# One decode block on one core: head pairs with interleaved K and V loads and a softmax per pair, in place of a K stage, one softmax for all heads and a V stage

## The chip, the cores and the metric

One core of one Trainium2 chip runs the kernel. The metric is the device time of one execution in microseconds (us), read as the median of several runs.

TensorE (the matmul engine) is PE in the profile, its weight load PEld, VectorE is DVE, ScalarE is ACT, GpSimd is POOL and SyncE, which issues most DMAs, is SP.

## The reference, cut to what matters

One token (a row of 640 numbers) goes through attention over a window of 4,096 cached positions with 32 heads of 192, then through a gated MLP.

```python
h  = x + A(layernorm(x));   h2 = h + B(layernorm(h))
def A(x):                     # 32 heads, Dh = 192, W = 4096
    q = (x @ wq)              # wq: 640 x 6144
    p = softmax(q @ k.T * Dh ** -0.5)     # k, v: the last W rows of each head's cache
    return (p @ v) @ wo       # wo: 6144 x 640
def B(x):                     # w_in 640 x 1536, w_out 768 x 640
    z = gelu(x @ w_in); z1, z2 = halves(z)
    return (z1 * (layernorm(z2) * w_sp + b_sp)) @ w_out
```

K and V of the window are 100.7 MB of the 119.35 MB that must be read. Each byte is used once, and the DMA engines were busy 95.5% of the span (kernel before), so this is a problem of reading memory.

## The kernel before

Each K or V tile holds one head: partition p has 32 consecutive positions of 192 numbers, 12,288 bytes in one piece. VectorE multiplies the K tile by the query, TensorE adds up the products with an identity matrix as weights, and scores of all 32 heads are collected. Only then come one maximum, one exponential and one sum for all heads, and after that the V stage. K and V tiles share five buffers.

```python
KVB = 5
kvp = ctx.enter_context(tc.tile_pool(name="kv", bufs=KVB))
...                                                   # plan of loads: x, wq and all K, then wo and all V, then w_in, w_out
for h in range(H):
    ...
    nc.vector.tensor_tensor(out=prod[:], in0=kt[:], in1=q_bc[:, h:h + 1, :].to_broadcast([P, J, Dh]), op=ALU.mult)
    for t in range(NT):                               # 12 matmuls of 512 columns
        nc.tensor.matmul(psv, lhsT=ident_bf[:], rhs=prod[:, :, t * G:(t + 1) * G], ...)
    nc.scalar.copy(out=spart[:, :, h % HH, :], in_=psv.rearrange("p j g -> p g j"))
...                                                   # max over all heads, exp, sums
for h in range(H):
    for jj in range(J // 2):                          # 16 matmuls of 384 columns
        nc.tensor.matmul(pv[0:2, 0:2 * Dh], lhsT=E_all[:, h, 2 * jj:2 * jj + 2], rhs=vt[:, 2 * jj:2 * jj + 2, :], ...)
    ...                                               # scaling, transposes, wo
...                                                   # MLP: h_col, w_in, gelu, layernorm, w_out
```

Of the kernel before, what the change touches and what calls it, by code (L numbers as in the profile page):

```python
# [9 lines left out]
F32 = mybir.dt.float32  # L10
ALU = mybir.AluOpType
# [5 lines left out]
def kernel(  # L17
# [19 lines left out]
    J = W // P  # L37
    DC = D // P
    F = B_w_in.shape[-1]
# [3 lines left out]
    DA = P  # L43
    DB = Dh - P
    assert W % P == 0 and D % P == 0 and Fh % P == 0 and 0 < DB <= P
    scale = float(Dh) ** -0.5
    eps = 1e-5

    G = 512 // J
    NT = Dh // G  # L50
    HH = min(H, 512 // J)
    assert Dh % G == 0 and H % HH == 0
    HG = 8 if H % 8 == 0 else H
    HQ = 8 if H % 8 == 0 else H
    WQC = HQ * Dh
    QB = 512 if WQC % 512 == 0 else 384
    assert WQC % QB == 0

    kwin = A_k_cache[0, :, Sk - W:, :].rearrange("h (p j) d -> h p j d", p=P)
    vwin = A_v_cache[0, :, Sk - W:, :].rearrange("h (p j) d -> h p j d", p=P)  # L60
    wq_v = A_wq.rearrange("(c p) n -> p c n", p=P)
    assert Dh == 192 and H % 2 == 0
    PPG = HG // 2
    wo_r = A_wo.rearrange("(q p i) n -> p q (i n)", p=P, i=3)
# [3 lines left out]
    I32 = mybir.dt.int32  # L68
    KVB = 5
    const = ctx.enter_context(tc.tile_pool(name="const", bufs=1))  # L70
    small = ctx.enter_context(tc.tile_pool(name="small", bufs=2))
    kvp = ctx.enter_context(tc.tile_pool(name="kv", bufs=KVB))
    wqp = ctx.enter_context(tc.tile_pool(name="wq", bufs=2))
    wop = ctx.enter_context(tc.tile_pool(name="wo", bufs=6))
    NSB = H // HH
    psum = ctx.enter_context(tc.tile_pool(name="psum", bufs=5, space=bass.MemoryType.PSUM))
    assert NSB <= 2
    psacc = ctx.enter_context(tc.tile_pool(name="psacc", bufs=1, space=bass.MemoryType.PSUM))
    o2p = ctx.enter_context(tc.tile_pool(name="o2", bufs=3))
    kctx = ExitStack()  # L80
    prodp = kctx.enter_context(tc.tile_pool(name="prod", bufs=2))
    psS = kctx.enter_context(tc.tile_pool(name="psS", bufs=NSB, space=bass.MemoryType.PSUM))

    def bank():
        return psum.tile([P, 512], F32, tag="bank", name="bank")

    NQC = H // HQ
    NG = H // HG
    tiles = {}
    x_row = const.tile([1, D], BF16)  # L90

    def dma_x():
        nc.sync.dma_start(out=x_row[:], in_=A_x[0])

    def dma_wq(ci):
        t = wqp.tile([P, DC, WQC], BF16, tag="wq", name="wq_sb")
        nc.sync.dma_start(out=t[:], in_=wq_v[:, :, ci * WQC:(ci + 1) * WQC])
        tiles[("wq", ci)] = t

    def dma_k(h):  # L100
        t = kvp.tile([P, J, Dh], BF16, tag="kv", name="kt")
        nc.sync.dma_start(out=t[:], in_=kwin[h])
        tiles[("k", h)] = t

    def dma_v(h):
        t = kvp.tile([P, J, Dh], BF16, tag="kv", name="vt")
        if h == H - 1 and J % 8 == 0:
            JQ = J // 4
            for qq in range(4):
                nc.sync.dma_start(out=t[:, qq * JQ:(qq + 1) * JQ, :], in_=vwin[h][:, qq * JQ:(qq + 1) * JQ, :])  # L110
        else:
            nc.sync.dma_start(out=t[:], in_=vwin[h])
        tiles[("v", h)] = t

    def dma_wo(qi):
        t = wop.tile([P, 3 * D], BF16, tag="woR", name="woR")
        nc.sync.dma_start(out=t[:], in_=wo_r[:, qi, :])
        tiles[("wo", qi)] = t

    def dma_win(c):  # L120
        if c == 0:
            wmlp = ctx.enter_context(tc.tile_pool(name="wmlp", bufs=1))
            tiles["w_in"] = wmlp.tile([P, DC, F], BF16, name="w_in_sb")
            tiles["w_out"] = wmlp.tile([P, FHC, D], BF16, name="w_out_sb")
        nc.sync.dma_start(out=tiles["w_in"][:, c, :], in_=win_v[:, c, :])

    def dma_wout():
        nc.sync.dma_start(out=tiles["w_out"][:], in_=wout_v)

    plan = [("x", 0, dma_x), ("wq", 0, lambda: dma_wq(0))]  # L130
    for h in range(H):
        if (h + 4) % HQ == 0 and (h + 4) // HQ < NQC:
            ci = (h + 4) // HQ
            plan.append(("wq", ci, lambda ci=ci: dma_wq(ci)))
        plan.append(("k", h, lambda h=h: dma_k(h)))
    NPAIR = H // 2
    for h in range(H):
        if h % 2 == 0 and h // 2 < NPAIR - 1:
            plan.append(("wo", h // 2, lambda qi=h // 2: dma_wo(qi)))
        plan.append(("v", h, lambda h=h: dma_v(h)))  # L140
    plan.append(("wo", NPAIR - 1, lambda: dma_wo(NPAIR - 1)))
    for c in range(DC):
        plan.append(("win", c, lambda c=c: dma_win(c)))
    plan.append(("wout", 0, dma_wout))
    plan_pos = {(k, i): n for n, (k, i, _) in enumerate(plan)}
    issued = [0]

    def need(kind, idx, ahead=KVB - 1):
        upto = min(len(plan), plan_pos[(kind, idx)] + 1 + ahead)
        while issued[0] < upto:  # L150
            plan[issued[0]][2]()
            issued[0] += 1

    need("wq", 0, ahead=2)
# [4 lines left out]
    ident_bf = const.tile([P, P], BF16)  # L159
    make_identity(nc, ident_bf[:])  # L160
    ident_f = const.tile([P, P], F32)
    make_identity(nc, ident_f[:])
# [8 lines left out]

    wsp_bf = const.tile([P, 1], BF16)
    nc.scalar.dma_start(out=wsp_bf[:], in_=B_w_sp[0].to_broadcast((P, 1)))
    bsp_bf = const.tile([P, 1], BF16)
    nc.scalar.dma_start(out=bsp_bf[:], in_=B_b_sp.to_broadcast((P, 1)))
    wsp_h = const.tile([P, 1], F32)
    nc.vector.tensor_scalar(out=wsp_h[:], in0=wsp_bf[:], scalar1=0.5, scalar2=None, op0=ALU.mult)
    bsp_h = const.tile([P, 1], F32)
    nc.vector.tensor_scalar(out=bsp_h[:], in0=bsp_bf[:], scalar1=0.5, scalar2=None, op0=ALU.mult)

# [30 lines left out]
    def ln_stats(T, C, avg_mat, eps_, iters):  # L211
        return ln_stats_b(ln_stats_a(T, C, avg_mat), eps_, iters)

    xc_ps = bank()
    for c in range(DC):
        nc.tensor.matmul(xc_ps[:, c:c + 1], lhsT=x_row[0:1, c * P:(c + 1) * P], rhs=ones_bf[0:1, 0:1],
                         start=True, stop=True)
    x_col = const.tile([P, 2, DC], F32)
    nc.vector.tensor_copy(out=x_col[:, 0, :], in_=xc_ps[:, 0:DC])
    mean1, rstd1 = ln_stats(x_col, DC, avgD_f, eps, 3)  # L220
    xn_bc = const.tile([P, DC, P], BF16)
    nc.vector.tensor_scalar(out=xn_bc[:], in0=x_col[:, 0, :, None].to_broadcast([P, DC, P]), scalar1=mean1,  # L222
                            scalar2=rstd1, op0=ALU.subtract, op1=ALU.mult)

    q_bc = const.tile([P, H, Dh], BF16)
    q_flat = q_bc[:].rearrange("p h d -> p (h d)")

    def q_chunk(ci):
        need("wq", ci, ahead=2)
        wq_sb = tiles.pop(("wq", ci))  # L230
        for nb in range(WQC // QB):
            ps = bank()
            for c in range(DC):
                nc.tensor.matmul(ps[:, 0:QB], lhsT=xn_bc[:, c, :], rhs=wq_sb[:, c, nb * QB:(nb + 1) * QB],  # L234
                                 start=(c == 0), stop=(c == DC - 1))
            col0 = ci * WQC + nb * QB
            nc.scalar.activation(out=q_flat[:, col0:col0 + QB], in_=ps[:, 0:QB], func=ACT.Copy, scale=scale)  # L237

    spart = prodp.tile([P, G, HH, J], BF16, tag="spart", name="spart", bufs=1)
    S_banks = []  # L240
    q_chunk(0)
    for h in range(H):
        if (h + 4) % HQ == 0 and (h + 4) // HQ < NQC:
            q_chunk((h + 4) // HQ)
        need("k", h)
        kt = tiles.pop(("k", h))
        prod = prodp.tile([P, J, Dh], BF16, tag="prod", name="prod")
        nc.vector.tensor_tensor(out=prod[:], in0=kt[:], in1=q_bc[:, h:h + 1, :].to_broadcast([P, J, Dh]),  # L248
                                op=ALU.mult)
        ps = bank()  # L250
        psv = ps[:, 0:J * G].rearrange("p (j g) -> p j g", j=J)
        for t in range(NT):
            nc.tensor.matmul(psv, lhsT=ident_bf[:], rhs=prod[:, :, t * G:(t + 1) * G],  # L253
                             start=(t == 0), stop=(t == NT - 1))
        nc.scalar.copy(out=spart[:, :, h % HH, :], in_=psv.rearrange("p j g -> p g j"))  # L255
        if h % HH == HH - 1:
            s_ps = psS.tile([P, 512], F32, tag="s_ps", name="s_ps")
            sv = s_ps[:, 0:HH * J].rearrange("p (a j) -> p a j", a=HH)
            for g_ in range(G):
# [128 lines left out]
    for pr in stage2:  # L388
        pair_wo(pr)
# [96 lines left out]
```

## Time and profile before

The median was 302.01 us over the first 4 runs (301.91 to 303.8).

| | before |
|---|---|
| read from memory | 119.35 MB, 395 GB/s over the span |
| DMA engines busy | 95.5% of the span |
| PE, DVE, ACT busy | 74%, 46%, 14% |
| last load (w_out) landed | 293.95 us |
| h_col (input of the MLP) written | 290.06 us |
| end of the span | 301.9 us |

The page of the kernel before. The rows of digits and of GB/s have 40 equal slices of the span; the line of percentages after the DMA queue is the chain of waits, followed back from the last instruction, by engine; a group line gives line, engine, operation, output and inputs, shapes, count, then busy us and mean ns, then the engine's idle time before it and what ended it:

```profile
span 301.9 us, 3098 instructions
...
DMA  5999999999999999999998899999999999999970
GB/s 169 423 435 399 436 416 420 418 420 431 417 421 408 427 431 417 423 431 417 425 419 352 314 414 431 425 417 422 425 423 416 418 426 429 422 420 419 394 264 2
...
q1 hardware_dynamic: 16092, 119.35, 95.5%
...
DMA 61%; PE 22%; DVE 13%; ACT 1%; issue 1%; ACTq 0%; DVEq 0%
...
L248 DVE TENSOR_TENSOR prod<-kt,q_bc 128x6144 bf16<-128x6144 bf16 x32 | 107.2, 3358 | 28.6 <-DMA kt<-in_A_k_cache_dram 23.0
...
L371 PE MATMUL bank<-vt,E_all 128*2 128x384 bf16 x512 | 89.9, 331 | 17.7 <-DMA vt<-in_A_v_cache_dram 17.7
```

DMA is at nine tenths in nearly every slice, and its queue holds 95.5% of the engines' time. The product (L248) is the large work of DVE; the values (L371) are two fifths of PE's 223.8 us. The exceptions are the first slice, the two slices from 158 to 174 us (352 and 314 GB/s) and the end. DVE does its product only in the first half of the span, and PE its value matmuls only in the second.

The windows view of the same kernel (per stretch: busy us and count of each engine, granted PE clock, DMA share, GB/s) tells the hole from the rest:

```profile
core 0: us, PE busy (x) PEld busy (x) DVE busy (x) ACT busy (x) POOL busy (x), PEclk, DMA share, GB/s
4.00:140.00 136.00, 100.19 (x426) 40.88 (x426) 103.90 (x50) 23.55 (x40) 0.00 (x0) 0.99 1.01 420
140.00:176.00 36.00, 28.07 (x136) 12.27 (x136) 14.28 (x19) 5.04 (x9) 0.00 (x0) 0.91 0.93 383
176.00:280.00 104.00, 82.37 (x526) 39.84 (x524) 12.24 (x38) 11.01 (x27) 0.00 (x0) 1.00 1.01 422
```

The DMA engines are full before and after the softmax of all heads and 0.93 full around it. A share a little over 1 is read here as full (1.01 beside 420 GB/s), so the GB/s beside it may be a few per cent high.

The timeline of the tail (start us, length us, engine, line, operation, output and inputs, shapes, count, then idle time before it) shows the values of the last head and h_col:

```profile
285.32 2.76 PE L371 MATMUL bank<-vt,E_all 128*2 128x384 bf16 x16
...
290.06 0.16 DVE L397 TENSOR_TENSOR h_col<-attn_ps,x_col 128x5 f32<-128x5 f32 x1 [0.60 <-PE attn_ps L357]
```

The values of the last head end at 288.1 us and h_col comes 2 us later; the 11.85 us from h_col to the end are the MLP.

### The profile page before, as it was taken

Reading aid. Unit: us, or ns where it says so; the run is one execution under the profiler, and the core shown is the slowest. Engines: PE = TensorE matmul, PEld = TensorE weight load, DVE = VectorE, ACT = ScalarE, POOL = GpSimd, SP = SyncE. Lnnn points to the kernel's source line nnn. Section 1 sums busy time; section 2 is a strip of 40 time slices with the busy share of each in tenths; the row PEclk is TensorE's granted clock in tenths of the full one; section 3 lists DMA queues with packets and bytes.
Section 4 is the critical chain, followed back from the end, with each engine's and each line's share of the span. In section 5 each row is a group of like instructions: output and inputs, shape, how many; then the busy total and the mean of one; then the engine's idle time right before and its main releaser. Section 6 shows DMA issues by size and latency. Waiting matters only on the chain.

```text
span 301.9 us, 3098 instructions
## 1 busy us (share of the span) xinstructions
PE 223.8 (74%) x1267; PEld 101.4 (34%) x1267; DVE 139.3 (46%) x157; ACT 42.7 (14%) x83; POOL 1.1 (0%) x9
## 2 busy tenths in 40 slices
PE   1377676786888977777767999888777677886952
PEld 0133232232333422233222544434333333343541
DVE  2397488947997598999624111110111011101154
ACT  1021311112111211111101111110111011102100
POOL 1000000000000000000000000000000000000000
PEclk9999999998899999999995999999999999999985
DMA  5999999999999999999998899999999999999970
GB/s 169 423 435 399 436 416 420 418 420 431 417 421 408 427 431 417 423 431 417 425 419 352 314 414 431 425 417 422 425 423 416 418 426 429 422 420 419 394 264 2
DMA packets 16395, 119.55 MB, mean 396 GB/s; under 512 B 1788, under 2 KB 2557, under 8 KB 8317
## 3 DMA queue, kind: packets, MB, share of 16 engines
q1 hardware_dynamic: 16092, 119.35, 95.5%
q8 instruction: 10, 0.16, 0.2%
q10 hardware_dynamic: 288, 0.00, 0.0%
q14 instruction: 5, 0.03, 0.0%
HBM read 119.34 MB, written 0.00 MB: 395 GB/s over the span
## 4 chain that ended last, share of the span: by engine, by line
DMA 61%; PE 22%; DVE 13%; ACT 1%; issue 1%; ACTq 0%; DVEq 0%
DMA kt<-in_A_k_cache_dram 35%; DMA vt<-in_A_v_cache_dram 24%; PE bank L371 15%; DVE prod L248 9%; DMA bsp_bf<-in_B_b_sp_dram 3%; PE rowA L333 2%; PE s_ps L260 1%; PE bank L253 1%; PE bank L234 1%; PE bank L309 0%; DVE lnt L204 0%; PE attn_ps L348 0%; DVE Sm L280 0%; DVE lny L207 0%; ACT E_all L284 0%
## 5 line engine op out<-in xcount | busy, mean ns | idle before, releaser
L248 DVE TENSOR_TENSOR prod<-kt,q_bc 128x6144 bf16<-128x6144 bf16 x32 | 107.2, 3358 | 28.6 <-DMA kt<-in_A_k_cache_dram 23.0
L253 PE MATMUL bank<-prod,ident_bf 128*128 128x512 bf16 x384 | 89.7, 385 | 30.4 <-DVE prod L248 30.4
L371 PE MATMUL bank<-vt,E_all 128*2 128x384 bf16 x512 | 89.9, 331 | 17.7 <-DMA vt<-in_A_v_cache_dram 17.7
L253 PEld LDWEIGHTS <-ident_bf 128*128 128x128 bf16 x384 | 35.9, 99 | 84.0 <-DVE prod L248 38.7
L371 PEld LDWEIGHTS <-E_all 128*2 128x2 bf16 x512 | 41.9, 85 | 61.7 <-DMA vt<-in_A_v_cache_dram 21.7
L384 DVE SCALAR_TENSOR_TENSOR o<-bank,RB,o2a 2x192 bf16<-2x192 f32 x32 | 13.0, 405 | 60.9 <-ACT o2a L383 59.2
L255 ACT CAST spart<-bank 128x512 bf16<-128x512 f32 x32 | 18.7, 585 | 105.6 <-PE bank L253 105.6
L383 ACT ACTIVATE o2a<-bank,RA 2x192 f32<-2x192 f32 x32 | 13.2, 411 | 113.1 <-PE bank L371 113.1
L311 DVE CAST o_sb<-bank 128x3 bf16<-128x3 f32 x16 | 2.6, 164 | 49.6 <-PE bank L309 49.6
L234 PE MATMUL bank<-wq_sb,xn_bc 128*128 128x512 bf16 x60 | 15.4, 415 | 5.5 <-DVE xn_bc L222 5.5
L333 PE MATMUL rowA<-woR,o_sb 128*1 128x512 bf16 x42 | 12.9, 378 | 3.3 <-DVE o_sb L311 3.3
L234 PEld LDWEIGHTS <-xn_bc 128*128 128x128 bf16 x60 | 6.2, 105 | 13.9 <-DVE xn_bc L222 5.6
L237 ACT ACTIVATE q_bc<-bank 128x512 bf16<-128x512 f32 x12 | 7.2, 597 | 17.8 <-PE bank L234 17.8
L336 PE MATMUL rowB<-woR,o_sb 128*1 128x128 bf16 x42 | 9.2, 219 | 0.0
L260 PE MATMUL s_ps<-spart,ident_bf 128*128 128x512 bf16 x32 | 7.2, 379 | 1.4 <-ACT spart L255 1.4
L333 PEld LDWEIGHTS <-o_sb 128*1 128x1 bf16 x42 | 3.5, 82 | 8.2 <-DVE o_sb L311 4.4
L260 PEld LDWEIGHTS <-ident_bf 128*128 128x128 bf16 x32 | 3.1, 98 | 5.5 <-issue 2.0
L266 DVE TENSOR_REDUCE m<-s_ps 128x16 f32<-128x512 f32 x2 | 1.4, 686 | 7.2 <-PE s_ps L260 7.2
L309 PEld LDWEIGHTS <-o 2*128 2x128 bf16 x48 | 2.4, 100 | 5.5 <-issue 5.0
L309 PE MATMUL bank<-ones_bf,o 2*128 2x1 bf16 x48 | 3.7, 166 | 0.5 <-DVE o L384 0.5
L336 PEld LDWEIGHTS <-o_sb 128*1 128x1 bf16 x42 | 3.5, 83 | 0.1
L185 PE MATMUL bank<-x_col,avgD_f 128*128 128x10 f32 x2 | 0.6, 376 | 3.7 <-DVE x_col L182 3.7
(86 smaller groups left out, 36.9 us busy)
## 6 DMA issues: line engine op xcount, KB each, us to landing
kt<-in_A_k_cache_dram SPq DMA_DIRECT2D x32, 1536.0 KB, 19.1
vt<-in_A_v_cache_dram SPq DMA_DIRECT2D x31, 1536.0 KB, 18.1
wq_sb<-in_A_wq_dram SPq DMA_DIRECT2D x4, 1920.0 KB, 14.3
woR<-in_A_wo_dram SPq DMA_DIRECT2D x16, 480.0 KB, 18.3
w_in_sb<-in_B_w_in_dram SPq DMA_DIRECT2D x5, 384.0 KB, 8.3
vt<-in_A_v_cache_dram SPq DMA_DIRECT2D x4, 384.0 KB, 14.8
w_out_sb<-in_B_w_out_dram SPq DMA_DIRECT2D x1, 960.0 KB, 9.9
wsp_bf<-in_B_w_sp_dram ACTq DMA_DIRECT2D x1, 0.2 KB
```

Source lines behind the costliest of these rows:

```text
L234: nc.tensor.matmul(ps[:, 0:QB], lhsT=xn_bc[:, c, :], rhs=wq_sb[:, c, nb * QB:(nb + 1) * QB], start=(c == 0), stop=(c == DC - 1))
L237: nc.scalar.activation(out=q_flat[:, col0:col0 + QB], in_=ps[:, 0:QB], func=ACT.Copy, scale=scale)
L248: nc.vector.tensor_tensor(out=prod[:], in0=kt[:], in1=q_bc[:, h:h + 1, :].to_broadcast([P, J, Dh]), op=ALU.mult)
L253: nc.tensor.matmul(psv, lhsT=ident_bf[:], rhs=prod[:, :, t * G:(t + 1) * G], start=(t == 0), stop=(t == NT - 1))
L255: nc.scalar.copy(out=spart[:, :, h % HH, :], in_=psv.rearrange("p j g -> p g j"))
L260: nc.tensor.matmul(sv, lhsT=ident_bf[:], rhs=spart[:, g_], start=(g_ == 0), stop=(g_ == G - 1))
L309: nc.tensor.matmul(o3_ps[:, i:i + 1], lhsT=o2f[:, i:2 * Dh:3], rhs=ones_bf[0:2, 0:1], start=True, stop=True)
L333: nc.tensor.matmul(rowA[0:1, 0:DA1], lhsT=pr["o3"][:, i:i + 1], rhs=woR[:, i * D:i * D + DA1], start=st_, stop=sp_)
L336: nc.tensor.matmul(rowB[0:1, 0:D - DA1], lhsT=pr["o3"][:, i:i + 1], rhs=woR[:, i * D + DA1:(i + 1) * D], start=st_, stop=sp_)
L371: nc.tensor.matmul(pv[0:2, 0:2 * Dh], lhsT=E_all[:, h, 2 * jj:2 * jj + 2], rhs=vt[:, 2 * jj:2 * jj + 2, :], start=(jj == 0), stop=(jj == J ...
L383: nc.scalar.activation(out=o2a[:], in_=pv[0:2, 0:Dh], func=ACT.Copy, scale=RA[:, h:h + 1])
L384: nc.vector.scalar_tensor_tensor(out=cur["o2"][:, hp, :], in0=pv[0:2, Dh:2 * Dh], scalar=RB[:, h:h + 1], in1=o2a[:], op0=ALU.mult, op1=ALU ...
```

## The change

The intent was to keep DMA full from start to end: give every stage the same mix of K and V work, close the hole at the softmax and use larger packets. Two heads share a tile (even partitions one head, odd partitions the other), so a row has 64 positions and 24,576 bytes. K and V loads alternate, K two pairs ahead. A manual schedule fixes the order of instructions: value work of pair t-2 stands after scores, maximum and exponential of pair t. The output projection uses 240 small matmuls in place of row matmuls, and the loads of w_sp and b_sp move from the start to the end. The diff, cut to its core:

```diff
-    kwin = A_k_cache[0, :, Sk - W:, :].rearrange("h (p j) d -> h p j d", p=P)
+    def pairs_of(cache, t):
+        return cache[0, 2 * t:2 * t + 2, Sk - W:, :].rearrange("h (p j) d -> p h (j d)", p=HALF)
-    wq_v = A_wq.rearrange("(c p) n -> p c n", p=P)
+    wq_v = A_wq.rearrange("(p c) n -> p (c n)", c=DC)
-    KVB = 5
+    KVB = 6
+    ctx.enter_context(tc.manual_schedule())
...
+    for t_ in range(NP):
+        if t_ + 2 < NP:
+            plan.append(("kv", lambda t=t_ + 2: dma_pair("k", A_k_cache, t)))
+        if t_ % 2 == 1:
+            plan.append(("wo", lambda q=t_ // 2: dma_wo(q)))
+        plan.append(("kv", lambda t=t_: dma_pair("v", A_v_cache, t)))
...
+    for t in range(NP + 2):
+        if t < NP:
+            S, m = scores(t)                 # 24 matmuls, 2 reductions
+        if ob_prev is not None:
+            columns(t - 3, ob_prev)
+        if t >= 4 and t % 2 == 0:
+            project((t - 4) // 2)
+        if t < NP:
+            gm = head_max(m)                 # transpose on PE, maximum on DVE
+            Z = exps(t, S, gm)               # broadcast on PE, exp on ACT
+        if t + 1 < NP:
+            for ch in range(NCH):
+                product(t + 1, ch)           # in place in the K tile
+        if t > 1:
+            ...
+            values(t - 2, vt, pv, 0, NJ)     # 32 matmuls
+            free("kv")
+            ob_prev = scaled(t - 2, pv)
+        if t < NP:
+            norms(t, Z)
...
+    nc.scalar.dma_start(out=wsp_bf[:, 0:1], in_=B_w_sp[0:1])     # was at the start
```

## The prediction

> **What bounds it now.** The DMA engines. By the windows view they are busy 0.99 of 4 to 140 us and 1.00 of 176 to 286 us, at 420 and 421 GB/s; the page gives 119.35 MB and 95.5% of 16 engines' span. DVE (46%) and PE (74%) are not the limit on average. DMA is not full in three places. First packets come 3.3 us after the start. Around 158 to 173 us (352 and 314 GB/s in the slices) the softmax of all heads runs alone and V buffers stay held: about 3.4 us of DMA is lost. After the last packet (about 293.4 us) 8.5 us of MLP follow; h_col is written at 290.06, 11.85 us before the end.
>
> **What the change does.** It handles heads in pairs (one on even, one on odd partitions), interleaves K and V loads and does a softmax per pair. Bytes stay the same, packets grow: a K or V row is 24,576 B, not 12,288; wq goes from 3,072 to 24,576 B, wo from 3,840 to 7,680.
>
> **Costs from the trace.**
> - Packets: the median 12,288 B packet took 464 ns, 3,072 B 125, 3,840 B 151. These fit 12 ns plus 27.2 B/ns [...]. Estimate for 24,576 B: 916 ns. Summed over 16 engines: 285 us before, 280 after: 4 to 5 us saved.
> - The softmax gap closes: 3.4 us saved.
> - Per pair, DVE: two products of 3.36, two PSUM reductions of 0.69, small ones 1.8: 9.9 us. PE: 24 score matmuls at 0.23, 32 value matmuls at 0.176, 1.2 for the rest: 12.5 us. The chain product, last scores, max, exp takes about 12.7. A pair's K and V take 14.7 us (17 with wo), and six buffers hold four loads ahead. So compute hides; DVE busy rises to about 155 us at no cost.
> - Start: q needs all of wq (21 us), then 80 matmuls, about 17 us; three K loads are in flight until 43 us, so DMA should not starve.
> - Tail, worse: value work lags two pairs. From the last K's landing (about 249 us): product 6.7, scores and softmax to 11.8, values 13, 14, 15 at 5.5 each with 1 to 2.5 us of scaling and projection between: to 32; h_col at 35, as late as the last DMA byte (34.6), where before it was 3.3 us ahead. The two tiny w_sp and b_sp loads move to the end of the scalar queue, ahead of h_col: 0 to 1.5 us more. In all 3 to 4 us given back.
>
> **Sum.** 302.0 - 4.5 - 3.4 - 0.8 (earlier first packet) + 3.5 = 296.8 us, range 293.5 to 300.5. Chances: faster by over 2% 0.40, within 2% 0.56, slower 0.04.
>
> **Signs.** DMA share 0.99 from 4 to 283 us without a hole in the middle, at 425 to 429 GB/s; K and V packets of 24,576 B at about 916 ns; last packet near 284 to 285 us; the chain of waits mostly DMA, with the last product and PE values at the end; h_col at about 285; PE waits 0 to 1.5 us for the w_sp load; 11 to 12 us from h_col to the end.
>
> **What would make it wrong.** Rows split into smaller packets, or no better rate for large ones: about 300. Two heads at once slowing HBM. A per-pair chain over 15 us (slow in-place product, PE waiting in program order for norms or transposes), so buffers come free late and DMA shows holes: 300 or more. A tail that overlaps better than I count: 294.

The two medians give both figures: from 3,072 B in 125 ns to 12,288 B in 464 ns it is 339 ns for 9,216 B, or 27.2 B/ns, and 12 ns are left over. The 916 ns stand on these alone.

## The result, and the profile after

The changed kernel took 300.92 us (median of 11 runs, 300.42 to 302.62), against 302.8 us for the kernel before (median of 16 runs, the first 4 among them). The ratio is 0.9951, 95% interval 0.9933 to 0.9968, a gain of about half a per cent. Ratios here are the mean time of one kernel's fast runs over that of the other's fast runs of the same rounds, so they are not quite the ratio of the medians. The predicted 296.8 us was too low by 4.1 us, and 300.92 lies just above the range. The time of a run is its span plus 1.7 to 1.9 us in every recorded run but one (2.1).

Lines of the page of the changed kernel: the span, the granted PE clock in tenths (PEclk), the GB/s, the DMA queue, the engines' shares of the chain of waits, and the groups of the product and the values:

```profile
span 298.9 us, 3737 instructions
...
PEclk9999995868999799989977998999989977999965
...
GB/s 306 431 421 444 434 426 429 420 431 437 417 425 440 423 441 424 423 437 420 431 437 414 434 431 417 437 431 421 418 444 423 434 431 427 428 421 398 293 2 0
...
q1 hardware_dynamic: 7930, 119.35, 94.0%
...
PE 64%; DMA 20%; DVE 12%; issue 1%; ACT 1%; SPq 0%; ACTq 0%; DVEq 0%
...
L240 DVE TENSOR_TENSOR k_t<-k_t,q 128x6144 bf16<-128x6144 bf16 x32 | 106.0, 3352 | 30.7 <-DMA k_t<-in_A_k_cache_dram 30.7
...
L292 PE MATMUL pv_ps<-v_t,E 128*4 128x384 bf16 x512 | 98.5, 358 | 0.0
```

The windows view of the changed kernel, same columns as before:

```profile
4.00:140.00 136.00, 103.53 (x587) 50.58 (x587) 76.76 (x104) 11.38 (x41) 0.00 (x0) 0.91 1.01 430
140.00:176.00 36.00, 33.54 (x215) 17.01 (x216) 23.89 (x30) 3.35 (x15) 0.00 (x0) 0.91 1.00 428
176.00:280.00 104.00, 88.56 (x627) 45.22 (x625) 54.05 (x77) 7.71 (x32) 0.00 (x0) 0.93 1.00 424
```

The product has kept its 3.4 us, in place or not; a value matmul takes 358 ns in the mean instead of 331. The hole is gone (1.00 and 428 GB/s where it was 0.93 and 383), and the rate is higher (430 GB/s from 4 to 140 us where it was 420). The DMA side of the prediction holds. In the packet records, packets of 24,576 B took 914 ns (median), where 916 was estimated. The w_out load landed at 284.31 us, 9.6 us earlier than before; the terms for DMA summed to 8.7. Of the 0.9 us more, 0.7 can lie at the start: the first packet of a large load came at 1.8 us instead of 3.3, where a gain of 0.8 was counted.

But from that landing to the end of the span it is now 14.6 us, where it was 8.0 us. So the tail gave back 6.6 us, not 3.5. The timeline of the changed kernel from the last but one K on:

```profile
235.47 6.63 DVE L240 TENSOR_TENSOR k_t<-k_t,q 128x6144 bf16<-128x6144 bf16 x2 [4.53 <-DMA k_t<-in_A_k_cache_dram]
...
238.88 7.03 PE L250 MATMUL sc_ps<-k_t,ident_bf 128*128 128x512 bf16 x24 [3.89 <-DVE k_t L240]
...
248.84 7.04 PE L292 MATMUL pv_ps<-v_t,E 128*4 128x384 bf16 x32
...
250.10 6.63 DVE L240 TENSOR_TENSOR k_t<-k_t,q 128x6144 bf16<-128x6144 bf16 x2
...
255.84 5.35 PE L250 MATMUL sc_ps<-k_t,ident_bf 128*128 128x512 bf16 x24
...
263.19 5.36 PE L292 MATMUL pv_ps<-v_t,E 128*4 128x384 bf16 x32
...
271.18 5.36 PE L292 MATMUL pv_ps<-v_t,E 128*4 128x384 bf16 x32
...
278.03 5.36 PE L292 MATMUL pv_ps<-v_t,E 128*4 128x384 bf16 x32
...
286.30 0.15 DVE L364 TENSOR_TENSOR h_col<-attn_ps,x_col 128x5 f32<-128x5 f32 x1
```

Read it as a chain on PE. The last K (pair 15) landed at 250.07 us by the landing records, and the first half of its product was done near 253.4. Yet its scores began at 255.84, because PE was still at the values of pair 12. From then on scores and three groups of values follow each other with gaps of 1.5 to 2.6 us, in which PE does small matmuls and waits for a maximum or a scaling. The last V landed at 277.01 us, and its values ended only at 283.4.

Two groups in these lines lasted about 7.0 us where their siblings took 5.36. The windows view of the changed kernel, same columns, in stretches of the length of the clock record's steps, shows why (the granted clock follows the counts of POOL):

```profile
235.80:239.20 3.40, 0.32 (x2) 0.19 (x2) 3.40 (x2) 0.00 (x0) 0.00 (x0) 0.99 1.06 455
239.20:242.60 3.40, 3.40 (x10) 1.22 (x8) 3.37 (x4) 0.00 (x0) 0.00 (x0) 0.51 0.94 405
...
246.00:249.40 3.40, 2.28 (x49) 1.83 (x48) 1.45 (x5) 0.20 (x1) 0.00 (x0) 1.00 0.97 411
249.40:252.80 3.40, 3.40 (x13) 1.33 (x12) 2.80 (x2) 0.57 (x4) 0.00 (x0) 0.50 1.06 447
```

After 3.4 us with 0.32 us of PE work, and again after 3.4 us with 2.28 us of it, the granted clock fell to half for the next 3.4 us; 5.36 us plus half of 3.4 us is 7.06 us, and the two groups took 7.03 and 7.04. Of the eleven half clock stretches in the clock record of this trace seven last 3.4 us and three 6.8 us; the last, from 286.9 us, runs to the end of the span. Why the clock falls was not shown. The mean granted clock was 0.967 before and 0.906 after.

### The profile page after: what moved, and what is told of

Read it like the earlier page. It is cut to its first block, busy times and chain, and to the rows that moved or that the text cites. A ratio compares the mean times of both kernels' runs of the same rounds, so it can differ in the third digit from the quotient of the medians.

```text
span 298.9 us, 3737 instructions
## 1 busy us (share of the span) xinstructions
PE 235.5 (79%) x1596; PEld 120.2 (40%) x1596; DVE 164.4 (55%) x266; ACT 24.7 (8%) x92; POOL 2.3 (1%) x10
## 4 chain that ended last, share of the span: by engine, by line
PE 64%; DMA 20%; DVE 12%; issue 1%; ACT 1%; SPq 0%; ACTq 0%; DVEq 0%
PE pv_ps L292 27%; PE sc_ps L250 26%; DMA k_t<-in_A_k_cache_dram 13%; DMA wq_t<-in_A_wq_dram 7%; PE sc_ps L226 5%; DVE k_t L240 3%; DVE S L252 3%; PE attn_ps L322 2%; PE sm_ps L267 2%; DVE gm L262 1%; PE sm_ps L260 1%; DVE m L255 1%; PE sm_ps L312 1%; DVE o L314 1%; ACT E L273 1%
## 5 line engine op out<-in xcount | busy, mean ns | idle before, releaser
L240 DVE TENSOR_TENSOR k_t<-k_t,q 128x6144 bf16<-128x6144 bf16 x32 | 106.0, 3352 | 30.7 <-DMA k_t<-in_A_k_cache_dram 30.7
L250 PE MATMUL sc_ps<-k_t,ident_bf 128*128 128x512 bf16 x384 | 90.7, 395 | 13.2 <-DVE k_t L240 13.2
L292 PE MATMUL pv_ps<-v_t,E 128*4 128x384 bf16 x512 | 98.5, 358 | 0.0
L292 PEld LDWEIGHTS <-E 128*4 128x4 bf16 x512 | 45.7, 92 | 46.7 <-issue 15.1
L252 DVE TENSOR_REDUCE S<-sc_ps 128x32 f32<-128x512 f32 x32 | 22.0, 688 | 41.7 <-PE sc_ps L250 41.7
L226 PE MATMUL sc_ps<-wq_t,xn 128*128 128x384 bf16 x80 | 17.6, 390 | 14.9 <-DMA wq_t<-in_A_wq_dram 14.9
L273 ACT ACTIVATE E<-S,bias 128x64 bf16<-128x64 f32 x32 | 11.2, 359 | 140.8 <-DVE bias L269 140.8
L226 PEld LDWEIGHTS <-xn 128*128 128x128 bf16 x80 | 9.1, 114 | 23.1 <-issue 16.0
L312 PEld LDWEIGHTS <-ob 4*32 4x32 bf16 x192 | 7.5, 134 | 9.4 <-issue 5.5
L312 PE MATMUL sm_ps<-sel,ob 4*32 4x1 bf16 x192 | 8.9, 184 | 3.0 <-DVE ob L300 3.0
```

Source lines behind the costliest of these rows:

```text
L226: nc.tensor.matmul(psv, lhsT=xn2[:, c, a, :], rhs=wc[:, 2 * gq:2 * gq + 2, a, :], start=(c == 0 and a == 0), stop=(c == DC - 1 and a == 1))
L240: nc.vector.tensor_tensor(out=kc, in0=kc, in1=q2[:, t:t + 1, :].to_broadcast([P, JC, Dh]), op=ALU.mult)
L250: nc.tensor.matmul(psv, lhsT=ident_bf[:], rhs=k3[:, ch * JC:(ch + 1) * JC, n * G:(n + 1) * G], start=(n == 0), stop=(n == NT - 1))
L252: nc.vector.tensor_reduce(out=S[:, ch * JC:(ch + 1) * JC], in_=psv, axis=AX.X, op=ALU.add)
L273: nc.scalar.activation(out=E[:, :, a], in_=S[:], func=ACT.Exp, bias=bias[:, a:a + 1], accum_out=Z[:, a:a + 1])
L292: nc.tensor.matmul(pv[0:4, 0:2 * Dh], lhsT=E[:, 2 * jj:2 * jj + 2, :], rhs=v2[:, jj, :], start=(jj == 0), stop=(jj == J // 2 - 1))
```

## The experiments

Two theories of the 4 us were on the table. The first: DMA paces the kernel up to the last loads, as predicted, and the loss sits in the tail, made of PE's program order and of half clock. The second, suggested by the chain view (PE 64%, DMA 20%): PE now paces the whole kernel, and the larger packets and the closed hole are worth nothing. A third suspicion was a wrong anchor, since the profile of before came from the slowest of its 16 runs. All runs were correct. They were made on three chips, each beside the kernel before, so they are best compared by their ratios.

### 1. The kernel before, once more (before_again)

No edit.

> The unchanged kernel of before, run again to learn its spread. Theory (wrong anchor): the profile of before that the prediction was computed from has a span of 301.9 us and came from a run timed at 303.8 us, while the median was 302.0 us; measured time is the span plus 1.8 us, so most runs of before should show spans near 300.2 to 301, and the predicted span of 296.8 us should have been quoted as 298.6 us. Rival (no anchor error): spans of before cluster at 301.9 us and the 303.8 us run is the odd one.

Measured: median 303.11 us of 4 runs, 302.29 to 303.38; ratio 1.0019, interval 0.9991 to 1.0046. Its spans were 300.5 to 301.6, and the kernel before, run beside it, had times of 301.48 to 303.55 us (11 runs). So the theory holds in its main point: time is span plus 1.8 or 1.9 us in each of these runs, and a span of 301.9 (time 303.8) is at the slow edge. The expected 300.2 to 301 was a little narrow. What makes one run of before slower than another by 1 to 2 us was not settled.

### 2. Small packets (small_packets)

```diff
-            nc.sync.dma_start(out=t[:], in_=src)
+            for a, b in ((J // 4, J // 2), (J // 2, 3 * J // 4), (3 * J // 4, J), (0, J // 4)):
+                nc.sync.dma_start(out=t[:, a * Dh:b * Dh], in_=src[:, :, a * Dh:b * Dh])
```

> Changed kernel with every K and V load cut into four DMAs of 6,144 B rows, the first quarter loaded last so that nothing can start earlier. Packets of 6,144 B took 236 ns and of 24,576 B 914 ns in the changed kernel, so a row costs 30 ns more and all rows 7.5 us more over 16 engines. If the DMA stream still paces the kernel up to the last K, the time rises by 6 to 7.5 us over the changed kernel (to about 307.5 us). If the chain of waits is right that PE (64%) now paces it, the time rises by under 2 us.

Measured: 307.09 us, ratio 1.0157 (1.0126 to 1.0188). Against the ratio of the changed kernel, 0.9951, that is 2.1% or 6.2 us more. Two lines of the page of this run, the GB/s and the DMA queue:

```profile
GB/s 310 422 414 412 418 421 416 421 413 419 415 418 419 412 418 415 416 417 417 416 417 416 418 417 416 417 417 416 417 421 412 417 420 415 418 421 415 351 11 0
...
q1 hardware_dynamic: 21322, 119.35, 95.4%
```

The rate fell to about 417 GB/s, and w_out landed at 291.62 instead of 284.31 us. So DMA still paces the kernel up to the last loads, and the second theory falls. The chain view gave PE 64% because it goes back from a load's landing to its issue, and from there to the PE work that freed the buffer. The one K load on that chain was issued at 196.33 us and landed at 235.44. It did not transfer for 39 us (at 430 GB/s its 3.1 MB take 7.3 us, by estimate): it stood in a full queue (DMA share 1.01 in that time). The same view gives softmax_late2 below DMA 55% and PE 30%, with loads that land at the same times.

### 3. Keeping PE busy in the tail (warm_tail)

```diff
+    def warm_pe(n):            # n dummy matmuls of 384 columns into a spare bank
+        wb = bank()
+        for _ in range(n):
+            nc.tensor.matmul(wb[:, 0:2 * Dh], lhsT=ident_bf[:], rhs=q2[:, 0:2, :], start=True, stop=True)
     for t in range(NP + 2):
+        if t == NP - 2:
+            warm_pe(22)
         if t < NP:
             S, m = scores(t)
+        if t >= NP:
+            warm_pe(5)
         if ob_prev is not None:
             columns(t - 3, ob_prev)
+        if NP - 2 <= t < NP:
+            warm_pe(5)
```

> Changed kernel with dummy matmuls in TensorE's idle stretches of the last four iterations (22 before the scores of pair 14, 5 in each later gap), the result unchanged. Theory (half clock matters): the scores of pair 14 and values of pair 12 ran at half clock (7.0 instead of 5.3 us) after idle stretches; with TensorE kept busy both run at 5.3 us and the time falls by 1.2 to 2 us. Rival (the order of the work alone sets the end, or the idle time is swallowed by waits): change under 0.4 us.

Measured: 299.39 us, ratio 0.9901 (0.988 to 0.9922), so 0.5% or 1.5 us less than the changed kernel. Its timeline has the dummies, the values of pair 12, and h_col:

```profile
235.81 3.75 PE L332 MATMUL sm_ps<-q,ident_bf 128*128 128x384 bf16 x22
...
248.24 5.36 PE L292 MATMUL pv_ps<-v_t,E 128*4 128x384 bf16 x32
...
285.24 0.15 DVE L376 TENSOR_TENSOR h_col<-attn_ps,x_col 128x5 f32<-128x5 f32 x1
```

The values of pair 12 took 5.36 us, not 7.04, and h_col came 1.06 us earlier, although the last K landed 0.4 us later (250.48 us). From that landing to h_col it is 34.8 us, where the changed kernel took 36.2. The clock record has no half clock between 220.1 and 285.0 us. Added PE work made the kernel faster. So half clock on the tail's chain cost about 1.5 us.

### 4. Deferring the softmax, first attempt (softmax_late)

In each iteration `values(t - 2)` was put ahead of columns, projection and maximum of pair t, and `exps` of pair t was moved to iteration t+1. The diff here and the next one are shortened to the calls.

```diff
         S, m = scores(t)
+        Z, E = exps(t - 1, ...)
+        product(t + 1)
+        nc.vector.tensor_copy(out=Z[:, 2:4], in_=Z[:, 0:2])
+        values(t - 2); scaled(t - 2)
         columns(t - 3); project(...)
-        gm = head_max(m); Z = exps(t, S, gm)
-        product(t + 1)
-        values(t - 2); scaled(t - 2)
-        norms(t, Z)
+        head_max(m)
+        norms(t - 1, Z)
```

> Changed kernel with another order of work in an iteration, no work added or taken: values of pair t-2 follow the scores of pair t at once on TensorE, and max, bias and exp of pair t are finished one iteration later, so TensorE has no wait of 2 to 3 us between scores and values. Theory (the tail is TensorE's backlog from waits in program order): values of the last pair end near 279.5 us instead of 283.4, h_col near 282.3 instead of 286.3, and the time falls by 3 to 4.5 us to about 297 us. Rival (the tail is bound by loads landing, last V at 277.0 and w_in at 281.9 us): under 1 us.

Measured: 303.98 us, ratio 1.0061 (1.0029 to 1.0093): 3 us slower than the changed kernel, so a miss. Its timeline shows the fault:

```profile
242.18 0.16 DVE L342 COPY Z<-Z 128x2 f32<-128x2 f32 x1
...
242.39 0.19 PE L279 MATMUL sm_ps<-ones_f,Z 128*4 128x1 f32 x2 [4.61 <-DVE Z L342]
...
242.51 8.09 PE L250 MATMUL sc_ps<-k_t,ident_bf 128*128 128x512 bf16 x24
```

The copy of Z (line 342) stood on DVE behind both products of pair 14, and PE's matmul for the norm (line 279), which needs it, stood ahead of the scores. So the scores began at 242.51 us, where the changed kernel began them at 238.88. Here two engines with a fixed order each made a wait of 4.61 us that neither order shows alone. The run tells nothing for or against the theory.

### 5. The same, with the order mended (softmax_late2)

```diff
         S, m = scores(t)
+        norms(t - 2, ...)          # needs a copy of Z made an iteration ago
+        columns(t - 3, ob_prev)
+        exps(t - 1, ...)
+        product(t + 1); copy of Z(t - 1)
+        values(t - 2); scaled(t - 2)
+        project(...)
+        head_max(m)
```

> The reordering of softmax_late, with its own fault mended: there the copy of Z stood behind the two products of the next pair on VectorE, and TensorE's matmul for the norm, which waits for that copy, stood ahead of the next scores, so the scores of pair 14 began at 242.5 instead of 238.9 us, after both products. Here norm and head columns of earlier pairs come right after the scores, nothing that TensorE does before the next scores waits for a product. Theory (order of work on TensorE makes the tail): scores of pair 15 end near 260 us, the last values near 279.5 us, h_col near 282.5 us, time 296 to 298 us. Rival (any deferral of the softmax costs as much as it gains, or the end is bound by landings): 300 us or more.

Measured: 297.62 us, ratio 0.9833 (0.9816 to 0.985), which is 1.2% or 3.6 us under the changed kernel by the ratios. Its timeline has the second half of the scores of pair 15, the values of pair 15 and h_col, near the expected 260, 279.5 and 282.5 us:

```profile
256.70 2.75 PE L250 MATMUL sc_ps<-k_t,ident_bf 128*128 128x512 bf16 x12 [0.52 <-DVE k_t L240]
...
274.30 5.36 PE L291 MATMUL pv_ps<-v_t,E 128*4 128x384 bf16 x32
...
282.58 0.15 DVE L371 TENSOR_TENSOR h_col<-attn_ps,x_col 128x5 f32<-128x5 f32 x1
```

The bytes, the arithmetic and the loads are the same; w_out landed at 284.45 us, as before the reordering (284.31), and the last K at 250.00 (250.07). So the order of work on PE in the tail, with the half clock on its chain, cost the changed kernel over 3 us. If half clock is put at the 1.5 us of warm_tail, the order alone is worth about 2 us, by estimate.

### 6. Tiny loads back to the start (late2_tail)

```diff
     nc.scalar.dma_start(out=x_row[:], in_=A_x[0])
+    nc.scalar.dma_start(out=wsp_bf[:, 0:1], in_=B_w_sp[0:1])          # and b_sp; was ahead of h_col
...                                # the negated mean computed inside the statistics, h2a ahead of the last c3
```

> softmax_late2 with the two tiny loads of w_sp and b_sp back at the start and two small VectorE instructions of the MLP tail moved into gaps. By the trace of the changed kernel TensorE waited for no tiny load (h_col 0.2 us after the last projection), and the MLP tail was 0.6 us longer than before by the order of small instructions: expected 0.3 to 0.8 us less than softmax_late2. If the tiny loads were a real cost at the tail, as the prediction allowed: 1 to 1.5 us less.

Measured: 297.05 us, ratio 0.9813 (0.9797 to 0.9829), 0.6 us less than softmax_late2. This is what the order of small instructions was estimated to be worth, not the 1 to 1.5 us of a late load. The run moved both together, but the profiles share it out. From h_col to the issue of the output store softmax_late2 took 10.43 us and this run 9.84, so the gain lies behind h_col, in the order of small instructions. From the start of the last projection to h_col only 0.2 us was saved. Its timeline has the values of pair 12, the second half of the scores of pair 15, the values of pair 15 and h_col:

```profile
247.13 5.36 PE L301 MATMUL pv_ps<-v_t,E 128*4 128x384 bf16 x32
...
257.06 2.75 PE L260 MATMUL sc_ps<-k_t,ident_bf 128*128 128x512 bf16 x12 [0.52 <-DVE k_t L250]
...
274.66 5.36 PE L301 MATMUL pv_ps<-v_t,E 128*4 128x384 bf16 x32
...
282.75 0.16 DVE L373 TENSOR_TENSOR h_col<-attn_ps,x_col 128x5 f32<-128x5 f32 x1 [0.98 <-PE attn_ps L331]
```

The scores of pair 15 now end near 259.8 us and the last values near 280.0. This is the fastest kernel.

### 7. Half clock where PE is not the last to arrive (late2_warm)

`warm_pe(30)` ahead of the scores of pair 14 in late2_tail, otherwise no change.

> late2_tail with 30 dummy matmuls in the idle stretch before the scores of pair 14. In late2_tail those scores still took 7.1 us at half clock, but the scores of pair 15 then waited for their product (until 253.8 us), not for TensorE. Theory (half clock costs only where TensorE is the last to arrive): scores of pair 14 near 6 us, time within 0.4 us of late2_tail. Rival (any half clock stretch costs about its lost time): 1 to 1.7 us less.

Measured: 297.57 us, ratio 0.9833 (0.9807 to 0.986). By the medians this is 0.5 us more than late2_tail, which was timed on another chip; the intervals of the ratios overlap. The rival's 1 to 1.7 us less are not seen, and the theory's bound of 0.4 us was just missed. The run is not clean either. Its timeline on PE has the scores of pair 14 in two halves and those of pair 15 in one line:

```profile
239.03 2.75 PE L260 MATMUL sc_ps<-k_t,ident_bf 128*128 128x512 bf16 x12 [0.42 <-DVE k_t L250]
242.30 2.75 PE L260 MATMUL sc_ps<-k_t,ident_bf 128*128 128x512 bf16 x12 [0.52 <-DVE k_t L250]
...
253.64 7.03 PE L260 MATMUL sc_ps<-k_t,ident_bf 128*128 128x512 bf16 x24 [1.42 <-DVE k_t L250]
```

The scores of pair 14 took 6.0 us instead of 7.1, but PE was then done earlier, waited longer, and the scores of pair 15 took 7.03 us, as long as the scores of pair 14 did at half clock in the changed kernel. The scores of pair 15 ended 0.9 us later than in late2_tail, and h_col came 0.9 us later (283.61 us). So, by these lengths, the dummies moved the half clock onto the chain rather than removed it, and whether half clock off the chain is free stays open.

### 8. The hole alone (before_deep)

```diff
-    KVB = 5
+    KVB = 7
-    wop = ctx.enter_context(tc.tile_pool(name="wo", bufs=6))
+    wop = ctx.enter_context(tc.tile_pool(name="wo", bufs=4))
```

> The kernel of before with seven instead of five K/V buffers (and four instead of six wo buffers to make room). It tests the price put on the hole at the softmax of all heads. Theory: two more buffers let DMA go on through 158 to 173 us, the GB/s there stay above 400, the last packet lands some 3 us earlier and the time falls by 2.5 to 3.4 us. Rival (the hole was free, because the end of the kernel of before is set by its own compute): hole gone, time within 1 us.

Measured: 299.76 us, ratio 0.9904 (0.9887 to 0.992). The GB/s of its page:

```profile
GB/s 193 419 431 406 426 423 426 411 421 431 420 422 404 432 426 423 422 422 426 429 413 425 417 411 418 431 418 426 416 429 416 422 426 427 420 422 420 395 286 2
```

The two slices that had the hole (the 22nd and 23rd) now read 425 and 417 GB/s, w_out landed at 290.94 instead of 293.95 us, and the time fell by 1% or 3.0 us beside 302.75. The hole was worth 3.0 us, where 3.4 was estimated. The two constants were changed together, and the first also lets loads run further ahead, so strictly this is the price of both. Two changed constants in the kernel before gained more than the whole rewrite.

## Why the prediction was wrong, point by point

**DMA bounds the kernel before: right.** The hole's price was 3.0 us by before_deep; 3.4 was predicted.

**Larger packets save 4 to 5 us: right in mechanism.** 914 ns against an estimated 916, and cutting the rows to 6,144 B cost 6.2 us of time. The estimate is the line through the medians of 3,072 and 12,288 B (125 and 464 ns), continued to 24,576 B. 16 engines with a packet of 24,576 B each in 916 ns would move 429 GB/s, and the trace has 430 from 4 to 140 us. Together with the hole and the earlier start, the last landing moved by 9.6 us where 8.7 was summed.

**Compute hides in the steady state: right.** No hole appeared in DMA, although DVE was busy for 164.4 us where 155 was predicted.

**"In all 3 to 4 us given back": this step failed.** The prediction put the last K at about 249 us and the way from there to the end at 47 us. The mechanism (values one after another on PE, then the MLP) was right; the sizes were short. The tail gave back 6.6 us (14.6 us after the last landing, 8.0 before). Against the prediction's own marks:

| step | predicted | measured | difference |
|---|---|---|---|
| last K lands | about 249 | 250.07 | +1.1 |
| from there to h_col | 35 | 36.2 | +1.2 |
| h_col to the end | 11.85 | 12.6 | +0.75 |

These marks add up to 295.85 us, 0.85 less than the 296.7 us that the prediction's terms give when they are taken from the 301.9 us of the profile; so the span was missed by the three differences, 3.05 us, less 0.85: the same 2.2 us as below. In the first row the sum of packet times was 1 us short (94.0% of 298.9 is 281.0 us, where 280 was estimated). The second is the half clock. The step of the chain that failed is "scores and softmax to 11.8": the values of pair 13 began 13.1 us after the last K, because the values of pair 12, which the prediction does not count behind the last K, still held PE, for 7.04 us where every group of values was taken for 5.5. From there to h_col the chain took 23.1 us where 23.2 was predicted. The prediction did not ask what clock PE would be granted after its waits. With that half clock gone, in warm_tail, the way from the last K to h_col was 34.8 us, which is the 35 predicted. The third is a slightly worse order of small DVE instructions in the MLP: from h_col to the issue of the output store the kernel before took 9.74 us, the changed kernel 10.36 and late2_tail 9.84. The two tiny loads, given 0 to 1.5 us, cost almost nothing: h_col was written 0.2 us after the last projection matmul.

**The anchor: this failed as well.** The savings and losses were read in a profile whose span of 301.9 us belonged to a run of 303.8 us, but they were subtracted from a median of 302.0. Subtracted from the span that they were read in, the same terms give a span of 296.7 us, which is a time of 298.5. The miss of 4.1 us thus has two parts of about the same size: 2.2 us of span (298.9 measured), which is the tail's 6.6 - 3.5 less the 0.9 us that DMA gained beyond its terms, and about 1.9 us of anchor. The second part is bookkeeping. Against the median of all 16 runs of before, 302.8 us, the base of 302.0 was only 0.8 us low, and the gain was 1.9 us by the medians (1.5 by the ratio) where 5.2 was forecast. What made the profiled run slow, and whether it swelled the terms that were read in it, stays open.

**What the prediction saw and did not use.** It listed the tail as PE values one after another, and named the risk of PE waiting in program order, but only for the steady state. softmax_late2 shows that in the tail this order, with its half clock, was worth over 3 us. Most of that is not part of the miss, as the predicted 35 us already held the values one after another; it is what the kernel could have had.

## What to carry to other kernels

When a change fills the queue of the limiting engine, find the last load that starts a long serial chain, here the last K, and add up that chain with its waits, not only its work; what follows the last load is paid in full (36.2 us from the last K to h_col and 14.6 us after the last landing in the changed kernel). In a chain with gaps, ask also what clock the matmuls behind the gaps will be granted (here 0.51 and 0.50 in two stretches of 3.4 us, about 1.5 us of time by warm_tail). Take durations from a profile, but check whether its run was typical, and do not mix its span with the median of times.

## What the traces show of the clock and of packets

- In the changed kernel a stretch of 3.4 us with 2.28 us of PE work in it, small matmuls included, and no idle time over 0.75 us was followed by half clock (0.50 granted from 249.4 to 252.8 us), as was a stretch with 0.32 us of work (0.51 granted from 239.2 to 242.6 us). Two stretches with 2.59 and 2.57 us of work (from 232.4 and from 259.6 us) were not (0.99 and 1.00 granted after them). What decides was not tested.
- 42 dummy matmuls in the waits of the tail made this kernel 1.5 us faster (warm_tail).
- For loads issued from SP the packet records of the two kernels have medians of 236 ns for 6,144 B, 460 (changed) and 464 (before) for 12,288 and 914 for 24,576. Beside the 27.2 B/ns worked out from the medians of 3,072 and 12,288 B that leaves 8 to 12 ns a packet, by estimate.
- With one core at work, the kernel before moved 420 GB/s from 4 to 140 us and the changed kernel 430.
